# Rewriting the start of a two-layer MLP kernel: the order of ten cells written out, eight weight buffers lent by the second layer, one exchange moved to DMA

## The chip, the cores and the metric

The kernel runs on one core of a Trainium2 chip. The metric is the device time of one execution in microseconds (us). Before the change it is 1242.22 us, the median of three runs (1239.99 to 1244.42).

## The reference, cut to what matters

Three steps follow one another on 2 x 4096 rows of 192 numbers, all in float32.

```
# 1. dynamic convolution: softmax over 7 taps, per row and head (8 heads of 24)
w = exp(weight_gen - max) / sum;  x_pad = 6 zero rows, then x
x1[b,s,h,:] = sum_k w[b,s,h,k] * x_pad[b, s+k, h, :]
# 2. first MLP, ELU          w_in 192x2048, w_out 2048x192
h = x1 @ w_in;   g = where(h > 0, h, exp(min(h, 0)) - 1);   x2 = g @ w_out
# 3. second MLP, hard swish
h = x2 @ w_in2;  g = h * clip(h + 3, 0, 6) / 6;             out = g @ w_out2
```

## The kernel before, in words

**Tiling.** The 8192 rows are cut into 16 blocks of 512. A block passes through a layer in eight cells; cell q multiplies the block by 256 of the 2048 hidden columns, applies the activation and multiplies by the matching 256 rows of the output weights. There are 2 x 16 x 8 = 256 cells, and `n` counts them. Every operand is split into a high and a low part, and a product is three products (high x high, high x low, low x high). A cell writes its first product into two PSUM banks, `h` (one set of two for even cells, one for odd cells). Its second product is accumulated in `acca` and `accb` by the matmuls of cell n+3 (`LAG`).

**One cell.** TensorE: first product of cell n, second product of cell n-3 (L515). ScalarE: two activations for each of the two banks (L537, L538), then a cast of both halves to the high part `gh` (L544). VectorE: one operation per bank to finish the activation (L554), then the low part `gl` (L548, on two SBUF tiles).

**The weights of the first layer.** They are prepared while the first ten cells run (`BOOT`). They come in 16 units of 128x384, i0 to i7 of `w_in` and o0 to o7 of `w_out`. Cell q needs unit i_q, and cell q+3 needs o_q. A unit is loaded into a `raw` buffer as pairs of 32-bit words that form float64 numbers. ScalarE takes the absolute value (`begin`, L147), VectorE makes five operations of it (`s0` to `s4`, L151 to L174), ScalarE casts the high part (`high`, L169), TensorE makes three matmuls for the rest (`p5`, L180 to L182) and ScalarE casts that to the low part (`p6`, L187). There are four raw buffers (`RAWS`). Unit k+4 is loaded once `s4` of unit k has read its buffer. From cell 3 on SyncE issues such a load only behind markers (L521) that wait for matmuls of the cell.

**Order.** All engines take their instructions in the order in which the code issues them. For the first ten cells this order comes from one string of letters for each cell (`scripts`): M the matmuls, x X y Y the activation of one and the other bank, R and G the high and low part of the cell before, 0 to 4, H, P, L the steps of the one or two units of this cell's `turn`, B the masks of the next. A digit issues the same step for both units.

**Convolution.** Block 0 is shared by VectorE and GpSimd, blocks 1 and on run on GpSimd (L279 to L302) once VectorE has made the softmax; L267 is its last step. `prepare` transposes the result, and makes the high part `xh` and the low part `xl`. Then one half of the partitions must be exchanged with the other: for block 0 by ScalarE (L337) and VectorE (L342), for all others by DMA (L346).

Of the kernel before, what the change touches and what calls it, by code (L numbers as in the profile page):

```python
# [8 lines left out]
F32 = mybir.dt.float32  # L9
F32R = mybir.dt.float32r  # L10
U32 = mybir.dt.uint32
# [6 lines left out]
def kernel(  # L18
# [62 lines left out]

    WI = [{k: cpool.tile([P, NQ * UN], F32R, name=f"wi{m}_{k}") for k in "hl"} for m in range(2)]

# [6 lines left out]

    def load_w(kind, m, q):
        raw = stage.tile([P, UN, 2], U32, tag="raw", name="raw", bufs=RAWS)
        if kind == "i":
            for k in range(2):
                c = (2 * q + k) * 2 * P
                src = w_in[m][:, c:c + 2 * P].rearrange("(g p) c -> p g c", p=HP)
                dst = raw[half[k]].rearrange("p (g c) b -> p g (c b)", g=3)
                if k == 0:
# [15 lines left out]
    class Unit:  # L114


        def __init__(self, kind, m, q, k=None):
            self.kind, self.m, self.q = kind, m, q
            self.raw = load_w(kind, m, q)
            self.hw, self.lw = self.raw[:, :, 1], self.raw[:, :, 0]  # L120
            if m == 0:

                c = k % 2 * UN
                self.f, self.rr = fts[k // 2 % 2][:, c:c + UN].bitcast(U32), boot[:, k * UN:(k + 1) * UN]

        def parts(self):
            m, q = self.m, self.q
            if self.kind == "i":
                cs = slice(q * UN, (q + 1) * UN)
                return WI[m]["h"][:, cs], [(WI[m]["l"][:, cs], slice(0, UN))], lambda t: t  # L130
# [186 lines left out]
    def prepare(m, i):  # L317
# [11 lines left out]
        else:  # L329
            parts = [(zin.pop(i)[:, 0:XN], lambda t: t[:, 0])]  # L330

        def split():
            for src, w in parts:
                nc.scalar.copy(w(X["h"]), src)
            if m == 0 and i == 0:
                for a in range(2):
                    nc.scalar.copy(X["h"][half[1 - a], 1], X["h"][half[a], 0].bitcast(F32))  # L337
            for src, w in parts:
                nc.vector.tensor_tensor(w(X["l"]), src, w(X["h"]).bitcast(F32), op=ALU.subtract)
            if m == 0 and i == 0:  # L340
                for a in range(2):
                    nc.vector.tensor_copy(X["l"][half[1 - a], 1], X["l"][half[a], 0].bitcast(F32))  # L342
                return
            for k in "hl":
                for a in range(2):
                    later(1 if m == 0 and i in (1, 2) else 2, X[k][half[1 - a], 1].bitcast(F32), X[k][half[a], 0].bitcast(F32))  # L346
        return split
# [107 lines left out]
    def second_product(n, k, bank):  # L455
# [10 lines left out]
        if not bank and n + LAG < EARLY:  # L466
            ops = ops[0::2][:2] + ops[4:] + ops[1:4:2]
# [25 lines left out]
    def matmuls(n):  # L493
# [10 lines left out]
        l0, l1 = first_product(n, 0), first_product(n, 1)  # L504
        if n < EARLY:
            x1 = first_product(n + 1, 1)[:2] if n == EARLY - 1 else []
            rows = [(0, a0), (6, b0), (10 if n >= LAG else 0, l0)], [(0, l1), (9, a1), (15, b1), (19, x1)]
        else:
            x1 = first_product(n + 1, 1)[:2]
            rows = [(0, b0), (4, a0), (10, l0)], [(0, l1[2:]), (7, b1), (11, x1), (13, a1)]  # L510
        plan = [
            (s + j, k, op) for k, runs in enumerate(rows) for s, ops in runs for j, op in enumerate(ops)]
        seen = [added.pop(i) for i in range(3, NB) if n == prep[0, i] - 1]
        for _, k, (o, w, r, st, sp, wait, tell) in sorted(plan, key=lambda e: e[:2]):
# [5 lines left out]
            if tell:  # L520
# [3 lines left out]
                if now > 2 and tell[1] == 1:  # L524

                    transfers(1 + k + (now < NQ))
        if now < 3:
            transfers(len(waiting))

# [83 lines left out]
    units = [(u[0], 0, int(u[1]), k) for k, u in enumerate("i0 i1 i2 i3 o0 i4 o1 i5 o2 i6 o3 i7 o4 o5 o6 o7".split())]  # L613
    turn = [[1, 2], [3, 4], [5, 6], [7, 8], [9, 10], [11, 12], [13], [14], [15], []]
    ends = {k: n for n, ks in enumerate(turn) for k in ks} | {0: -1}
    close = [[1], [2]] + turn[1:-1]
    boards = [(aux, accb), acca, (aux, acca[1]), (aux, acca[1]), (None, None), (None, None)] + 4 * [(aux,)]
# [21 lines left out]
    begin = {i: max(7, prep[0, i - 1]) for i in range(2, NB)}  # L639
    loads = {max(2, begin[i] - 8): i for i in begin}  # L640
    softmax = {}

    three = cpool.tile([P, 1], F32, name="three")
    with tc.manual_schedule():
        nc.vector.memset(three, 3.0)
        nc.scalar.activation(warm, three, AF.Exp)
        def make(k):
            made[k] = Unit(*units[k])
# [5 lines left out]
        blk[1] = load_block(1)  # L654
        for k in (1, 2, 3):
            make(k)

        def start(n):
            for k, bank in zip(turn[n], boards[n]):
                made[k].masks(bank)  # L660

# [9 lines left out]
        for s in c0[5:]:  # L671
            s()
        c1 = attention(1)
        for s in c1[:4]:
            s()
        prepare(0, 0)()
        start(0)
        for s in c1[4:]:
            s()
        wst = Stream(wtasks)  # L680
        for n in range(len(cells) + LAG):
            now = n
            jobs = []
            if n < BOOT:
                for k in range(len(made), len(units)):
                    if ends[k - RAWS] < n:
                        make(k)
            for m, i in order:
# [4 lines left out]
                if m and i < NB - 1 and n == last[m, i] + LAG + 3:  # L693
                    jobs.append(give(i))
            if n < BOOT:
                new, old = [made[k] for k in turn[n]], [made[k] for k in close[n]]
                spare = hset[(n + 1) % 2][::-1][-len(old):] if n > 1 else [(aux, accb)[n]]
                work = {
                    "M": lambda: matmuls(n),
                    "R": lambda: round_g(n - 1), "G": lambda: rest_g(n - 1),  # L700
                    "H": lambda: [u.high() for u in new],
                    "x": lambda: act_a(n, 1), "X": lambda: gate(n, 1),
                    "y": lambda: act_a(n, 0), "Y": lambda: gate(n, 0),
                    "J": lambda: [f() for f in jobs],
                    "P": lambda: [u.p5(ps) for u, ps in zip(old, spare)],
                    "L": lambda: [u.p6() for u in old],
                    "B": lambda: start(n + 1) if n + 1 < BOOT else None}
                work |= {str(k): (lambda k: lambda: [getattr(u, f"s{k}")() for u in new])(k) for k in range(5)}
                for step in scripts[n]:
                    work[step]()  # L710
            else:
                matmuls(n)
                for k in (1, 0):
                    if n < len(cells):
                        act_a(n, k)
                        gate(n, k)
                    if not k:
                        continue
                    for b in order[:-1]:
                        if n == last[b] + LAG:  # L720
                            fold_b(*b)
                    if n <= len(cells):
                        round_g(n - 1)
                        rest_g(n - 1)
                    for b in order[:-1]:
                        if n == last[b] + LAG + 1:
                            fold_a(*b)
                for f in jobs:
                    f()
            if n == BOOT:  # L730
                want(0)
            wst.run(n)
            for i in range(2, NB):

                k = n - (begin[i] - 5) - (i == 2)
                if k == 0:
                    softmax[i] = attention(i)
                if 0 <= k < 4:
                    softmax[i].pop(0)()
                if n == begin[i]:  # L740
                    for s in softmax.pop(i):
                        s()
            if n < 3:
                transfers(len(waiting))
            if n in loads:
                blk[loads[n]] = load_block(loads[n])
        finish()
# [30 lines left out]
```

## Time and profile before

| | |
|---|---|
| median of three runs | 1242.22 us |
| profiled execution | 1237.81 us, of which the span of the core's instructions is 1236.0 |
| busy share of the span | TensorE 96%, VectorE 76%, ScalarE 69%, GpSimd 34% |
| mean granted TensorE clock | 0.991 of full speed |

All rows below are of this one execution, and times in them count from the start of its span. In a timeline row the bracket at the end is the idle time of that engine just before the instruction, and what ended it. A wait for several things is put down to the one that came last.

### The profile page before, as it was taken

The numbers are of one execution on the slowest core, as the hardware profiler recorded it, in microseconds if no ns is written. First come the engines' busy times: TensorE is split into PE (matmuls) and PEld (weight loads), VectorE is DVE, ScalarE is ACT, GpSimd is POOL, SyncE is SP. The second block draws the span as 40 slices with busy tenths as digits, with TensorE's granted clock in tenths as the row PEclk, the third lists the DMA queues.
The fourth block names the chain that finished last, engine by engine and source line by source line (L and its number), as shares of the span: only waits on it lengthen the run. The fifth ranks groups of instructions, "written<-read, shape, count | busy, mean of one in ns | idle before, by whom it ended". The sixth has DMA issues, their size and how long they took to land.

```text
span 1236.0 us, 25367 instructions
## 1 busy us (share of the span) xinstructions
PE 1191.7 (96%) x10146; PEld 946.1 (77%) x10146; DVE 938.8 (76%) x1225; ACT 856.7 (69%) x1339; POOL 416.8 (34%) x234
## 2 busy tenths in 40 slices
PE   3788999999999999999999999999999999999998
PEld 1466777777877777787788888888888888888887
DVE  7865899999999999999777666666666666666664
ACT  3656788888888888888886555566655556666554
POOL 8416877777787777778000000000000000000000
PEclk9899999999999999999999999999999999999999
DMA  5331222212222221221121011111111111111110
GB/s 135 112 103 37 88 88 88 68 43 66 88 88 88 88 66 39 71 88 53 52 65 45 21 52 52 47 45 52 33 33 53 52 50 42 53 33 33 52 40 27
DMA packets 33254, 75.03 MB, mean 61 GB/s; under 512 B 4340, under 2 KB 17010, under 8 KB 33136
## 3 DMA queue, kind: packets, MB, share of 16 engines
q1 hardware_dynamic: 32992, 73.21, 20.4%
q8 instruction: 80, 1.31, 0.4%
q14 instruction: 38, 0.31, 0.1%
q10 hardware_dynamic: 144, 0.20, 0.0%
HBM read 36.43 MB, written 12.58 MB: 40 GB/s over the span
## 4 chain that ended last, share of the span: by engine, by line
PE 92%; DVE 4%; DMA 2%; ACT 2%; issue 0%; SPq 0%; DVEq 0%; ACTq 0%
PE h L515 42%; PE acca L515 28%; PE accb L515 19%; DMA raw<-in_moe_w_out_dram 1%; DVE gl L548 1%; PE acca L327 1%; DMA xt<-in_x_dram 1%; DVE r L554 1%; ACT r L538 0%; PE acca L413 0%; ACT r L537 0%; PE acca L485 0%; DVE h L279 0%; DVE f L158 0%; PE accb L485 0%
## 5 line engine op out<-in xcount | busy, mean ns | idle before, releaser
L515 PE MATMUL h<-xh,wi_h 64*128 64x512 f32 x1536 | 566.7, 397 | 13.6 <-ACT wi_l L187 12.2
L515 PE MATMUL h<-xh,wi_l 64*128 64x512 f32 x1536 | 568.6, 397 | 0.0
L515 PE MATMUL h<-xl,wi_h 64*128 64x512 f32 x1536 | 564.3, 395 | 0.0
L515 PE MATMUL acca<-gh,wo 64*128 64x512 f32 x2024 | 560.5, 395 | 0.0
L548 DVE TENSOR_TENSOR gl<-r,gh 128x1024 fp32r<-128x1024 f32 x256 | 393.9, 1539 | 61.6 <-ACT gh L544 60.6
L515 PEld LDWEIGHTS acca<-gh,wo 64*128 64x128 f32 x2024 | 375.8, 186 | 47.9 <-issue 1.0
L540 ACT ACTIVATE r<-h,three 128x512 f32<-128x512 f32 x256 | 176.1, 688 | 222.7 <-PE h L515 113.2
L515 PE MATMUL accb<-gh,wo 64*128 64x512 f32 x1012 | 321.6, 397 | 5.5 <-ACT wo L187 5.5
L515 PEld LDWEIGHTS h<-xh,wi_h 64*128 64x128 f32 x1536 | 284.4, 187 | 52.1 <-ACT wi_l L187 13.4
L515 PE MATMUL acca<-gl,wo 64*128 64x512 f32 x1012 | 318.7, 394 | 0.0
L515 PE MATMUL accb<-gl,wo 64*128 64x512 f32 x1012 | 318.2, 394 | 0.3 <-DVE gl L548 0.3
L515 PEld LDWEIGHTS h<-xl,wi_h 64*128 64x128 f32 x1536 | 284.3, 186 | 35.7
L515 PEld LDWEIGHTS h<-xh,wi_l 64*128 64x128 f32 x1536 | 284.3, 186 | 35.5
L557 DVE SCALAR_TENSOR_TENSOR r<-r,h 128x512 f32<-128x512 f32 x256 | 175.9, 687 | 161.2 <-ACT r L540 160.4
L544 ACT CAST gh<-r 128x1024 fp32r<-128x1024 f32 x256 | 266.8, 1042 | 12.7 <-DVE r L554 11.9
L554 DVE SCALAR_TENSOR_TENSOR r<-r,h 128x512 f32<-128x512 f32 x256 | 173.3, 677 | 53.8 <-ACT r L538 52.2
L515 PEld LDWEIGHTS accb<-gh,wo 64*128 64x128 f32 x1012 | 185.8, 186 | 27.0 <-ACT wo L187 6.5
L515 PEld LDWEIGHTS accb<-gl,wo 64*128 64x128 f32 x1012 | 187.8, 186 | 24.0 <-DVE gl L548 0.7
L515 PEld LDWEIGHTS acca<-gl,wo 64*128 64x128 f32 x1012 | 188.1, 186 | 23.4
L279 POOL TENSOR_TENSOR tmp<-xt,wt 128x768 f32<-128x768 f32 (+1 forms) x95 | 189.3, 1992 | 6.1
L537 ACT ACTIVATE r<-h 128x512 f32<-128x512 f32 x256 | 152.4, 595 | 49.9 <-PE acca L515 30.6
L538 ACT ACTIVATE r<-r 128x512 f32<-128x512 f32 x256 | 162.0, 633 | 8.1
(134 smaller groups left out, 747.8 us busy)
## 6 DMA issues: line engine op xcount, KB each, us to landing
xt<-in_x_dram SPq DMA_DIRECT2D x14, 960.0 KB, 5.6
xh<-xh SPq DMA_DIRECT2D x62, 192.0 KB, 2.7
xl<-xl SPq DMA_DIRECT2D x62, 192.0 KB, 2.9
raw<-in_moe_w_out_dram SPq DMA_DIRECT2D x16, 384.0 KB, 3.3
z<-z SPq DMA_DIRECT2D x16, 384.0 KB, 2.3
zin<-z SPq DMA_DIRECT2D x16, 384.0 KB, 3.0
out_dram<-ot SPq DMA_DIRECT2D x15, 384.0 KB, 4.3
raw<-in_moe_w_in_dram SPq DMA_DIRECT2D x16, 192.0 KB, 3.4
```

The lines of the kernel that those rows point to most:

```text
L279: eng.tensor_tensor(o.rearrange("p t (h g) -> p t h g", g=G), xk, wk.rearrange("p (t h) g -> p t h g", h=H), op=ALU.mult)
L327: nc.tensor.transpose(ps[h][:, t * HP:(t + 1) * HP], src[p], ident[p, p])
L515: mm = nc.tensor.matmul(o, w, r, start=st, stop=sp).ins
L537: nc.scalar.activation(r, h, AF.Relu, scale=-1.0)
L538: nc.scalar.activation(r, r, AF.Exp, scale=-1.0)
L540: nc.scalar.activation(r, h, AF.Relu, bias=three)
L544: nc.scalar.copy(gg[n][0], rs[n])
L548: nc.vector.tensor_tensor(gl, rs.pop(n), gh.bitcast(F32), op=ALU.subtract)
L554: nc.vector.scalar_tensor_tensor(r, r, -1.0, h, op0=ALU.add, op1=ALU.max)
L557: nc.vector.scalar_tensor_tensor(r, r, 6.0, h, op0=ALU.min, op1=ALU.mult)
```

## The change

**Order.** The letters per cell are replaced by one list for the ten cells (`SCRIPT`), whose tokens name the step and its unit or cell: C5.2 is step s2 of unit 5, B5, H5, P5, L5 are its masks, high part, matmuls and low part, M4, x4, X4, y4, Y4, R4, G4 belong to cell 4, s1a to sC are softmax steps, T1, J, j are the transposes, high parts and low parts of block 1, wh and wl those of block 0. Steps of two or three units now stand in turns. `masks` and `sums` name the PSUM bank of each unit.

**Buffers.** Units 4 to 11 get buffers of their own, in the place where the second layer's input weights will lie later. The loads of units 4 to 7 are issued before cell 0, those of 8 to 11 right behind the exchange of `xl`, those of 12 to 15 at cell 2 into the four raw buffers. None stands behind a marker.

**Exchange.** The exchange of block 0's `xl` is two DMAs in SyncE's queue in place of two VectorE casts; that of `xh` stays on ScalarE.

**Matmuls.** In cells 8 and 9 the first and second product are interleaved as in the cells before them, where they followed the pattern of the later cells.

```diff
+    early = [cpool.tile([P, 4 * UN, 2], U32, tag=f"wi1{k}", name=f"early_{k}") for k in "hl"]
...
-    def load_w(kind, m, q):
-        raw = stage.tile([P, UN, 2], U32, tag="raw", name="raw", bufs=RAWS)
+    def load_w(kind, m, q, k=None):
+        if k is None or not RAWS <= k < RAWS + 8:
+            raw = stage.tile([P, UN, 2], U32, tag="raw", name="raw", bufs=RAWS)
+        else:
+            c = (k - RAWS) % 4 * UN
+            raw = early[(k - RAWS) // 4][:, c:c + UN]
...
-                for a in range(2):
-                    nc.vector.tensor_copy(X["l"][half[1 - a], 1], X["l"][half[a], 0].bitcast(F32))
...
+        def swap(keys, put):
+            for k in keys:
+                for a in range(2):
+                    put(X[k][half[1 - a], 1].bitcast(F32), X[k][half[a], 0].bitcast(F32))
...
-        if now is None or now >= len(cells) or now < 3 and n == 0:
+        if now is None or now >= len(cells) or now < BOOT and n == 0:
             nc.sync.dma_start(out, in_)
...
-    scripts = ["M012H34xXyYPLB", "MPR01xX2LyYH34GB", "MR01xX2yYH34GPLB"] + (BOOT - 3) * ["MR012H34GxXJByYPL"]
+    masks, sums = "xxbaccxcx----ccc", "xxbfbedgfedxcxxx"
+    SCRIPT = """
+        s1a B2 B1 C2.0 e1 C1.0 wh0 s1b wh1 wh2 wl0 s1c wh3 wl1 C2.1 B4 M0 C1.1 B3 C2.2 C4.0 H2 C1.2 C4.1 H1
+        C1.3 C3.0 C1.4 C4.2 P1 x0 C3.1 C4.3 C3.2 L1 M1 C4.4 y0 C2.3 X0 B5 C2.4 B6 Y0 P2 x1 C5.0 C6.0 y1 C3.3
...
+    """
...
-        for k in (1, 2, 3):
+        for k in range(1, 8):
             make(k)
...
+            elif t[:2] == "wl":
+                split[0].rest(int(t[2]))
+                if t == "wl1":
+                    split[0].swap("l", nc.sync.dma_start)
+                    for k in range(8, RAWS + 8):
+                        make(k)
```

SyncE's queue before the change: the last piece of unit 3's load, then unit 4, unit 5 in three pieces, unit 6, and so on as buffers come free.

```order
L579 DMA raw<-in_moe_w_in_dram 64x256
L579 DMA raw<-in_moe_w_out_dram 128x2x384
L579 DMA raw<-in_moe_w_in_dram 64x3x256
L579 DMA raw<-in_moe_w_in_dram 64x2x256
L579 DMA raw<-in_moe_w_in_dram 64x256
L579 DMA raw<-in_moe_w_out_dram 128x2x384
```

The same place after the change, where `early_h` holds units 4 to 7.

```order
L598 DMA raw<-in_moe_w_in_dram 64x256
L598 DMA early_h<-in_moe_w_out_dram 128x2x384
L598 DMA early_h<-in_moe_w_in_dram 64x3x256
L598 DMA early_h<-in_moe_w_in_dram 64x2x256
L598 DMA early_h<-in_moe_w_in_dram 64x256
L598 DMA early_h<-in_moe_w_out_dram 128x2x384
L598 DMA early_h<-in_moe_w_in_dram 64x3x256
L598 DMA early_h<-in_moe_w_in_dram 64x2x256
L598 DMA early_h<-in_moe_w_in_dram 64x256
L357 DMA xl<-xl 64x768 x2
L598 DMA early_l<-in_moe_w_out_dram 128x2x384
```

Three more units are loaded ahead of cell 0's end, and the exchange of `xl` stands behind them and in front of four more.

VectorE after the low parts of block 0, before the change: the two casts, then units 1 (`aux`) and 2 (`accb`) step by step.

```order
L339 TENSOR_TENSOR xl<-acca_77,xh 128x384
L342 CAST xl<-xl 64x768 x2
L151 TENSOR_SCALAR aux<-aux 128x384
L151 TENSOR_SCALAR accb<-accb 128x384
L154 TENSOR_SCALAR aux<-aux 128x384
L154 TENSOR_SCALAR accb<-accb 128x384
L158 SCALAR_TENSOR_TENSOR f<-raw,aux 128x384
L158 SCALAR_TENSOR_TENSOR f<-raw,accb 128x384
```

The same place after the change.

```order
L352 TENSOR_TENSOR xl<-acca_77,xh 128x384
L165 TENSOR_SCALAR accb<-accb 128x384
L165 TENSOR_SCALAR aux<-aux 128x384
L169 SCALAR_TENSOR_TENSOR f<-raw,accb 128x384
L162 TENSOR_SCALAR acca_77<-acca_77 128x384
L169 SCALAR_TENSOR_TENSOR f<-raw,aux 128x384
L165 TENSOR_SCALAR acca_77<-acca_77 128x384
L174 TENSOR_SCALAR aux<-f 128x384
L162 TENSOR_SCALAR acca_76<-acca_76 128x384
L185 SCALAR_TENSOR_TENSOR boot<-raw,aux 128x384
```

The casts are gone, and steps of units 4 (`acca_77`) and 3 (`acca_76`) stand between those of 1 and 2.

VectorE around the last softmax step of block 2 (L267, which lets GpSimd begin that block), before the change; the first `gl` here is cell 5's.

```order
L548 TENSOR_TENSOR gl<-r,gh 128x1024
L554 SCALAR_TENSOR_TENSOR r<-r,h_73 128x512
L554 SCALAR_TENSOR_TENSOR r<-r,h_72 128x512
L267 TENSOR_TENSOR wt<-wt,mx 128x224
L151 TENSOR_SCALAR aux<-aux 128x384
```

The same step after the change (now L278); the `gl` here is cell 3's.

```order
L352 TENSOR_TENSOR xl<-aux,xh 128x384
L573 SCALAR_TENSOR_TENSOR r<-r,h_72 128x512
L278 TENSOR_TENSOR wt<-wt,mx 128x224
L162 TENSOR_SCALAR tr<-tr 128x384 x2
L567 TENSOR_TENSOR gl<-r,gh 128x1024
```

The step stood behind the `gl` of cell 5, and now stands ahead of that of cell 3.

## Rows read from the trace of the kernel before

**Rows 1.** Windows: length, busy per engine, PEclk the granted clock, DMA share, GB/s.
```profile
40.00:50.00 10.00, 5.01 (x24) 3.50 (x25) 10.00 (x17) 7.16 (x14) 4.99 (x4) 0.66 0.55 190
20.90:116.58 95.68, 73.42 (x434) 51.45 (x436) 69.14 (x120) 59.21 (x114) 47.76 (x28) 0.89 0.25 77
181.10:217.30 36.20, 36.20 (x320) 28.89 (x318) 34.09 (x43) 30.33 (x51) 27.25 (x15) 1.00 0.25 75
```
**Rows 2.** Waits of VectorE, 20.9 to 116.6 us: total, times, longest.
```profile
DVE r L554 <- ACT r L538: 23.5, 10, 5.5
```
**Rows 3.** Timeline of VectorE: start, length, operation, idle time before it.
```profile
57.81 0.69 DVE L554 SCALAR_TENSOR_TENSOR r<-r,h 128x512 f32<-128x512 f32 x1 [2.76 <-ACT r L538]
...
70.02 0.69 DVE L554 SCALAR_TENSOR_TENSOR r<-r,h 128x512 f32<-128x512 f32 x1 [5.50 <-ACT r L538]
...
79.57 0.69 DVE L554 SCALAR_TENSOR_TENSOR r<-r,h 128x512 f32<-128x512 f32 x1 [2.54 <-ACT r L538]
...
96.95 0.69 DVE L554 SCALAR_TENSOR_TENSOR r<-r,h 128x512 f32<-128x512 f32 x1 [4.82 <-ACT r L538]
...
115.16 0.69 DVE L554 SCALAR_TENSOR_TENSOR r<-r,h 128x512 f32<-128x512 f32 x1 [3.05 <-ACT r L538]
```
**Rows 4.** Timeline of ScalarE, first and last of the masks that wait.
```profile
54.72 0.55 ACT L147 ACTIVATE tr<-raw 128x384 f32<-128x384 f32 x1 [1.54 <-DMA raw<-in_moe_w_in_dram]
...
95.22 0.52 ACT L147 ACTIVATE aux<-raw 128x384 f32<-128x384 f32 x1 [4.66 <-DMA raw<-in_moe_w_out_dram]
```
**Rows 5.** Timeline of SyncE's queue: start and length of issues.
```profile
6.47 10.65 SPq L579 DMA_DIRECT2D raw<-in_moe_w_in_dram  x9
...
50.15 2.73 SPq L588 DMA_DIRECT2D raw<-in_moe_w_in_dram  x3
```
**Rows 6.** Waits of SyncE's queue, up to 130 us.
```profile
SPq L521 <- PE acca L515: 40.1, 17, 7.3
```
**Rows 7.** Timeline of VectorE in cells 0 and 1.
```profile
22.06 2.74 DVE L342 CAST xl<-xl 64x768 fp32r<-64x768 f32 x2
...
30.60 0.69 DVE L554 SCALAR_TENSOR_TENSOR r<-r,h 128x512 f32<-128x512 f32 x1 [0.43 <-ACT r L538]
...
35.52 0.69 DVE L554 SCALAR_TENSOR_TENSOR r<-r,h 128x512 f32<-128x512 f32 x1 [1.14 <-ACT r L538]
```
**Rows 8.** Timeline of VectorE: the low part of cells 1 and 8.
```profile
47.47 1.21 DVE L548 TENSOR_TENSOR gl<-r,gh 128x1024 fp32r<-128x1024 f32 x1
...
106.69 2.62 DVE L548 TENSOR_TENSOR gl<-r,gh 128x1024 fp32r<-128x1024 f32 x1 [0.17 <-ACT gh L544]
```
**Rows 9.** Timeline of GpSimd: first and last of block 2's 14 operations, first of block 3's.
```profile
87.41 1.54 POOL L279 TENSOR_TENSOR y<-xt,wt 128x768 f32<-128x768 f32 x1 [42.26 <-DVE wt L267]
...
112.02 0.74 POOL L302 TENSOR_TENSOR y<-y,tmp 128x256 f32<-128x256 f32 x1
126.07 1.83 POOL L279 TENSOR_TENSOR y<-xt,wt 128x768 f32<-128x768 f32 x1 [13.31 <-PE aux L327]
```
**Rows 10.** Windows of the first loads.
```profile
10.00:20.00 10.00, 3.17 (x14) 1.78 (x14) 8.85 (x19) 0.87 (x2) 8.55 (x10) 1.00 0.97 213
20.00:30.00 10.00, 5.51 (x26) 3.37 (x25) 9.66 (x17) 6.13 (x12) 8.74 (x5) 0.95 0.05 15
```
**Rows 11.** DMA issues up to 170 us: KB each, median us to landing.
```profile
xl<-xl SPq DMA_DIRECT2D x4, 192.0 KB, 3.1
```
**Rows 12.** Timeline of TensorE: the weight matmuls of units 1, 2 and 15; cells 0 and 2.
```profile
21.41 0.80 PE L515 MATMUL h<-xh,wi_h 64*128 64x512 f32 x2 [0.94 <-ACT xh L334]
...
29.16 1.65 PE L180 MATMUL aux<-f,ident 128*128 128x384 f32 x2 [3.06 <-DVE boot L174]
...
34.11 0.91 PE L180 MATMUL accb<-f,ident 128*128 128x384 f32 x2
...
35.30 0.50 PE L515 MATMUL h<-xh,wi_h 64*128 64x512 f32 x2
...
110.02 0.91 PE L180 MATMUL h<-f,ident 128*128 128x384 f32 x2
```

More of the change, by code (lines that the diff above doesn't have):

```diff
@@ L330, in prepare, with cast, turn, rest @@
             parts = [(zin.pop(i)[:, 0:XN], lambda t: t[:, 0])]
-        def split():
-            for src, w in parts:
-                nc.scalar.copy(w(X["h"]), src)
-            if m == 0 and i == 0:
-                for a in range(2):
[L337 to L341, printed above, removed]
-                    nc.vector.tensor_copy(X["l"][half[1 - a], 1], X["l"][half[a], 0].bitcast(F32))
[L343 to L346, printed above, removed]
+        def cast(k):
+            src, w = parts[k]
+            nc.scalar.copy(w(X["h"]), src)
+        def turn(a):
+            nc.scalar.copy(X["h"][half[1 - a], 1], X["h"][half[a], 0].bitcast(F32))
+        def rest(k):
+            src, w = parts[k]
+            nc.vector.tensor_tensor(w(X["l"]), src, w(X["h"]).bitcast(F32), op=ALU.subtract)
+        def swap(keys, put):
+            for k in keys:
+                for a in range(2):
+                    put(X[k][half[1 - a], 1].bitcast(F32), X[k][half[a], 0].bitcast(F32))
+        def split():
+            for k in range(len(parts)):
+                cast(k)
+            for k in range(len(parts)):
+                rest(k)
+            swap("hl", lambda o, t: later(1 if (m, i) == (0, 2) else 2, o, t))
+        split.cast, split.turn, split.rest, split.swap = cast, turn, rest, swap
         return split
@@ L639 @@
     begin = {i: max(7, prep[0, i - 1]) for i in range(2, NB)}
-    loads = {max(2, begin[i] - 8): i for i in begin}
+    loads = {begin[i] - 8: i for i in begin if i > 2}
     softmax = {}
@@ L672, with products @@
             s()
[L673 to L679, printed above, removed]
+        c1, split = attention(1), {0: prepare(0, 0)}
+        def products(n):
+            nonlocal now
+            if n:
+                trail(n - 1)
+            now = n
+            if n == 2:
+                blk[2] = load_block(2)
+                for k in range(RAWS + 8, len(units)):
+                    make(k)
+            matmuls(n)
+            if n == begin[2]:
+                for s in softmax.pop(2):
+                    s()
@@ new lines, in trail, with special @@
+        def trail(n):
+            for i in range(2, NB):
+                k = n - (begin[i] - 5)
+                if i > 2 and k == 0:
+                    softmax[i] = attention(i)
+                if i > 2 and 0 <= k < 4:
+                    softmax[i].pop(0)()
+                if i > 2 and k == 5:
+                    for s in softmax.pop(i):
+                        s()
+            if n in loads:
+                blk[loads[n]] = load_block(loads[n])
+        def special(t):
+            if t == "T1":
+                split[1] = prepare(0, 1)
+            elif t in ("s1a", "e1", "s1b"):
+                c1.pop(0)()
+            elif t == "s1c":
+                for s in c1:
+                    s()
+            elif t == "J":
+                split[1].cast(0)
+                split[1].cast(1)
+            elif t == "j":
+                split[1].rest(0)
+                split[1].rest(1)
+                split[1].swap("hl", nc.sync.dma_start)
+            elif t[:2] == "wh":
+                k = int(t[2])
+                (split[0].turn if k > 1 else split[0].cast)(k % 2)
+            elif t[:2] == "wl":
[3 more added lines that the diff above has]
+                    for k in range(8, RAWS + 8):
+                        make(k)
+            else:
+                if t == "sA":
+                    softmax[2] = attention(2)
+                softmax[2].pop(0)()
@@ new lines @@
+        plain = {
+            "M": products, "R": round_g, "G": rest_g,
+            "x": lambda n: act_a(n, 1), "y": lambda n: act_a(n, 0), "X": lambda n: gate(n, 1), "Y": lambda n: gate(n, 0),
+            "H": lambda k: made[k].high(), "L": lambda k: made[k].p6(), "P": lambda k: made[k].p5(banks[sums[k]]),
+            "B": lambda k: made[k].masks(banks.get(masks[k]))}
+        for t in SCRIPT.split():
+            if t[0] == "C":
+                k, p = t[1:].split(".")
+                getattr(made[int(k)], "s" + p)()
+            elif t[0] in plain and t[1:].isdigit():
+                plain[t[0]](int(t[1:]))
+            else:
+                special(t)
@@ L680 @@
+        trail(BOOT - 1)
         wst = Stream(wtasks)
-        for n in range(len(cells) + LAG):
+        for n in range(BOOT, len(cells) + LAG):
             now = n
             jobs = []
[L684 to L687, printed above, removed]
             for m, i in order:
@@ L694 @@
                     jobs.append(give(i))
[L695 to L729, printed above, removed]
+            matmuls(n)
+            for k in (1, 0):
+                if n < len(cells):
+                    act_a(n, k)
+                    gate(n, k)
+                if not k:
+                    continue
+                for b in order[:-1]:
+                    if n == last[b] + LAG:
+                        fold_b(*b)
+                if n <= len(cells):
+                    round_g(n - 1)
+                    rest_g(n - 1)
+                for b in order[:-1]:
+                    if n == last[b] + LAG + 1:
+                        fold_a(*b)
+            for f in jobs:
+                f()
             if n == BOOT:
@@ L732 @@
             wst.run(n)
[L733 to L746, printed above, removed]
+            trail(n)
         finish()
```

45 lines of the change are left out of this document (25 added, 20 removed).

## The prediction

> **What bounds the kernel now.** I read the windows first. From 181.10 to 217.30, cells 24 to 31, TensorE is busy all 36.20 us at granted clock 1.00: eight cells at 4.53 us, and nothing but fewer matmuls would shorten them [rows 1]. The change leaves those cells alone. The stretch that it rewrites is the one from 20.90 to 116.58, from the first split of block 0 to the low part `gl` of cell 9. There TensorE is busy 73.42 of 95.68 us at a mean clock of 0.89, ScalarE 59.21, VectorE 69.14 [rows 1]. No engine is full, so an order with less waiting can be shorter, and VectorE sits idle for 95.68 - 69.14 = 26.5 us.
>
> Then the waits of VectorE: 23.5 us of that idle time, in ten pieces, stand before the last step of an activation (L554) and end with ScalarE's L538 [rows 2]. ScalarE isn't slow there, it is late. Its timeline shows it standing in front of the masks of a weight unit until the raw words land, in four cells, at 54.72 first and at 95.22 last [rows 4]; the activation behind it in the queue waits too. On VectorE these four waits are the pieces of 2.76, 5.50, 2.54 and 4.82 us, together 15.6 [rows 3].
>
> Why the words are late stands on SyncE. From cell 3 on a load is issued behind markers that wait for matmuls (40.1 us on `acca` alone, [rows 6]), and only when one of four buffers is free: unit 9 at 50.15 [rows 5], though the DMA engines were nearly unused from 20 to 30 us (15 GB/s, [rows 10]).
>
> **The change part by part.** The yardstick is the start of `gl` of cell 9, 116.58, since the 69 us of VectorE work before it are the same in both orders but for the casts. Behind it both kernels run the same order.
>
> *Loads.* Units 4 to 15 are issued without a marker, 4 to 7 before cell 0. Three more units than before come right behind one another, 3 x 0.39 MB. The engines moved 213 GB/s at a share of 0.97 from 10 to 20 us, and 0.15 MB were left after 20 [rows 10]; so these units are in by 20 + (1.18 + 0.15)/0.213 = 26 us, and the next four, 1.57 MB, by about 37 with the exchange between. The 20 steps of units 1 to 4, some 0.5 us each, fill VectorE past 30 us together with the activations of cells 0 and 1, so the words are early from there on, and the four waits go: 15.6 us less. Could they come back? Only if a unit were wanted before it is in; the tightest is unit 5 (masks behind the activations of cell 0, after 30 us).
>
> *Exchange.* The two casts held VectorE for the 2.66 us from 22.06 to the next operation at 24.72, one of 2.74 in the row [rows 7]: 2.7 less. Two DMAs take their place, and their price is a wait on TensorE: the last matmuls of cell 0 need them, and the matmuls of unit 1, the activation of cell 0 and all that is queued behind these on ScalarE and VectorE stand behind. They are issued behind units 4 to 7. The bounds: they start at 23 us, when `xl` is ready, and land at 26.1 with the 3.1 us of such a DMA [rows 11]; or they start when the units are in, and land at 29.3. Unit 1's matmuls started at 29.16 before, held by VectorE [rows 12]; without the casts they could start at 26.5. So the DMA costs between 0 and (29.3 + 1 for the last matmuls - 26.5) = 4 us. I take the middle, 2, since both the backlog and the early start are in the rows.
>
> *Order on VectorE.* Of the 23.5 us, 15.6 are the loads; 0.43 and 1.14 stand in cells 0 and 1 [rows 7]; the other 6.3 come after 79 us, and most of them end late, the last and longest (3.05, [rows 3]) at 115.16, when only few weight steps are left and VectorE waits for a TensorE that was held up by the same loads. In the new order weight steps last until cell 9's products, and TensorE isn't behind; I let the 6.3 go. The 1.6 in the first cells, and the 3.0 that are left of the 26.5, I leave: a list for three engines must wait somewhere, and the bounds are that all of it goes, or that as much comes in addition.
>
> *GpSimd's block 2.* Its first operation waits for VectorE's L267 and it runs from 87.41 to 112.76, 25.3 us [rows 9]. While it runs, `gl` takes 2.62 us (cell 8), against 1.21 without it (cell 1) [rows 8], 1.41 more. L267 stood behind the `gl` of cell 5, so three of them (cells 6 to 8) ran beside block 2; it now stands ahead of that of cell 3, so six do. Three more cost 3 x 1.41 = 4.2 us; the bounds are nothing, if they fall between GpSimd's operations, and twice that, if GpSimd is drawn out too and reaches cell 9's.
> The Trainium skill speaks against this part more sharply: "SBUF — State Buffer", section "SBUF: two separate sides", says that a VectorE operation with two SBUF inputs and a GpSimd operation share a port pair by an exclusive lock, and that the loser waits for the other's whole instruction. `gl` reads two SBUF tiles, and the 1.41 is of the size of one GpSimd operation (1.54, [rows 9]), so the trace agrees. By the lock the eight SBUF steps of units 9 to 12 can be held as well, up to 8 x 1.54 = 12 us, and the gain would be 18.4 - 12 = 6.
>
> *What is hidden.* Units' steps done in turns save VectorE nothing that counts. The two reordered cells have the same matmuls. Second-layer weights come into the lent buffers only after cell 10, when unit 11 is long done. All three at nothing; they are hidden by TensorE's and VectorE's other work, and if unit 11 were late, its steps would show it first.
>
> *The sum.* 15.6 + 2.7 + 6.3 - 2.0 - 4.2 = 18.4 us earlier at cell 9. Does it last? From cell 24 on TensorE is full, so cells come as much earlier as cell 10 does, provided that block 2 of the convolution (wanted in cell 13) and block 3 are not the next to be late: block 2 ended at 112.76 and GpSimd then waited 13.3 us for TensorE to take it [rows 9]; it now starts earlier within the order, so this slack stays. The profiled execution took 1237.81; 1237.8 - 18.4 = 1219.4. The median of the three runs lies 4.4 above that execution, and I carry this over: 1223.8.
>
> **The rivals.**
> 1. *TensorE becomes the bound.* Cells 3 to 9 take 7 x 4.53 us, cells 0 to 2 have 9 of 19 pairs of matmuls, 3 x 2.15, and the 15 units' matmuls take 35.30 - 34.11 = 1.19 each, 17.9: together 56 us from 21.41 [rows 1, 12]. Cell 10 could begin at 77.5; it began at 110.02 + 1.19 = 111.2. So the floor of a perfect list is 34 us lower. For it speaks that all 26.5 us of idle VectorE would have to go, against it that VectorE alone still has 69 - 2.7 us of work: at most 26.5 + 2.7 = 29 us of gain, 1213. A gain of 24 to 29: 1213 to 1218.
> 2. *The waits change places.* The loads' waits go, but a list that ties three engines step by step hands on every delay; the late 6.3 stay, the exchange costs its 4, block 2 its 8.4. Then 15.6 + 2.7 - 4 - 8.4 = 6, or 1236; with one of the three not so bad 7 to 13, 1229 to 1235. For it speaks that VectorE then has 69.1 - 2.7 + 8.4 = 75 us of work and ScalarE 59, in 90.
> 3. *The loads stay late.* If the one queue is held up so that units 8 to 15 are as late as before, nothing is won: 1238 to 1246. Against it: no marker stands ahead of them, and the engines were idle.
> 4. *Slower: TensorE stays at its low clock.* From 40 to 50 us, with TensorE idle half of the time, the granted clock was 0.66 [rows 1], that is 1.2 GHz for most of it. If the new list makes short waits in every cell, TensorE can stay there. The 56 us at a mean clock c take 56/c; they reach the 111.2 - 21.4 = 89.8 us of before at c = 0.62, and below that the kernel is slower: at 0.55 by 102 - 90 = 12 us, 1254. Against it: with much idle time the mean was 0.89 [rows 1]. "TensorE: Matmul & The Clock Gate", section "HAM oscillation", of the Trainium skill says that bursts of matmuls between waits can each begin cold, which is this rival's mechanism; the trace shows it in that one stretch.
>
> **How the numbers follow.** The forecast, a gain of 13 to 24: 0.60. Rival 1: 0.10. Rival 2: 0.18. Rival 3: 0.06. Rival 4: 0.06. The best case of the bounds adds 2 + 4.2 + 4.6 to 18.4, beyond rival 1's limit of 29, so the low end is 1213; the upper end takes in rival 2 up to 1236, which leaves out rivals 3 and 4 and a little of the two ends. A measurement of this kernel can't tell less than about 0.3%, 3.7 us, from no change. Faster: 0.60 + 0.10 + 0.17 = 0.87; same: the rest of rival 2 and most of rival 3, 0.06; slower: 0.07.
>
> **What would show it.** Right: no wait of ScalarE for `raw` after 30 us; `gl` of cell 9 near 98; VectorE idle about 10 us up to it; the DMAs of `xl` landing between 26 and 29.5; `gl` of cells 3 to 8 at 2 us and more; an unchanged 36 us for eight cells later. Wrong: waits for `raw` that persist (rival 3), a granted clock under 0.7 up to cell 10 (rival 4), or waits of VectorE for ScalarE that add up to 20 us with no load behind them (rival 2).

## The result and the profile after

The changed kernel takes 1227.59 us, the median of four runs (1226.06 to 1228.03), against 1241.87 for the kernel before beside it (four runs, 1239.99 to 1244.42). The ratio is 0.9881, with a 95% interval of 0.9862 to 0.9901: 14.3 us faster. The two profiled executions are 1237.81 and 1227.44, which is 10.4 apart; the kernel before scatters by several us, and its profiled execution was one of the quicker ones. All that follows about where time went is on the scale of the profiled executions.

The low part `gl` of cell 9 starts at 105.94 instead of 116.58, 10.64 us earlier, and the last cell's is as much earlier (10.54). The whole difference is made in the first ten cells, and nothing is given back later.

Windows of the changed kernel; columns as in [rows 1], which they answer.

```profile
20.90:105.94 85.04, 69.71 (x434) 46.31 (x436) 75.62 (x122) 58.11 (x114) 48.28 (x28) 0.96 0.35 93
20.00:30.00 10.00, 4.20 (x18) 2.27 (x18) 9.40 (x22) 5.62 (x11) 6.40 (x5) 1.00 1.07 243
30.00:40.00 10.00, 9.26 (x45) 5.66 (x46) 5.92 (x13) 6.80 (x14) 9.61 (x6) 1.00 1.09 292
62.57:80.47 17.90, 10.14 (x53) 6.14 (x51) 17.90 (x18) 7.13 (x14) 16.97 (x10) 0.87 0.36 106
177.00:213.20 36.20, 36.20 (x320) 28.90 (x318) 34.12 (x43) 30.33 (x50) 27.29 (x15) 1.00 0.25 76
```

Read the first row against the 95.68 us of before. VectorE was idle for 26.5 us and is now idle for 85.04 - 75.62 = 9.4: 17.1 us less, close to what was forecast. But it is busy for 75.62 us instead of 69.14, though the two casts of 2.7 us are gone. So some 9 us of VectorE work have appeared that no instruction was added for (0.9 us of it are four softmax steps of block 1, which ran ahead of 20.90 before). The fourth row says where to look: from 62.57 to 80.47 VectorE is busy without a gap, with only 18 instructions, while TensorE has work for 10.14 of 17.90 us.

The timeline of VectorE in that stretch (start, length, operation; between the two `gl` stand the steps of units 11, 12 and 13, x2 is two steps in one row, `tr` is a mask tile in SBUF, `acca` one in PSUM):

```profile
63.11 2.57 DVE L567 TENSOR_TENSOR gl<-r,gh 128x1024 fp32r<-128x1024 f32 x1
65.59 3.62 DVE L165 TENSOR_SCALAR tr<-tr 128x384 uint32<-128x384 uint32 x2
69.14 1.90 DVE L169 SCALAR_TENSOR_TENSOR f<-early_l,tr 128x384 uint32<-128x384 uint32 x1
70.96 0.55 DVE L162 TENSOR_SCALAR acca<-acca 128x384 f32<-128x384 f32 x1
71.42 1.70 DVE L169 SCALAR_TENSOR_TENSOR f<-raw,tr 128x384 uint32<-128x384 uint32 x1
73.04 0.55 DVE L165 TENSOR_SCALAR acca<-acca 128x384 uint32<-128x384 uint32 x1
73.51 1.23 DVE L174 TENSOR_SCALAR tr<-f 128x384 uint32<-128x384 uint32 x1
74.66 0.54 DVE L169 SCALAR_TENSOR_TENSOR f<-raw,acca 128x384 uint32<-128x384 uint32 x1
75.13 1.71 DVE L185 SCALAR_TENSOR_TENSOR boot<-early_l,tr 128x384 fp32r<-128x384 uint32 x1
76.76 0.55 DVE L174 TENSOR_SCALAR acca<-f 128x384 uint32<-128x384 uint32 x1
77.22 1.23 DVE L174 TENSOR_SCALAR tr<-f 128x384 uint32<-128x384 uint32 x1
78.38 0.54 DVE L185 SCALAR_TENSOR_TENSOR boot<-raw,acca 128x384 fp32r<-128x384 uint32 x1
78.84 1.70 DVE L185 SCALAR_TENSOR_TENSOR boot<-raw,tr 128x384 fp32r<-128x384 uint32 x1
81.06 1.96 DVE L567 TENSOR_TENSOR gl<-r,gh 128x1024 fp32r<-128x1024 f32 x1
```

The same four operations (L165, L169, L174, L185) stand here with either tile, turn by turn: with `acca` they take 0.55, with `tr` 1.2 to 1.9. Beside them GpSimd is at block 2, whose first and last operation are these (the bracket is the idle time before it; L278, which the block needs too, had ended at 62.65):

```profile
62.87 1.72 POOL L290 TENSOR_TENSOR y<-xt,wt 128x768 f32<-128x768 f32 x1 [15.89 <-PE accb L536]
...
88.54 0.73 POOL L313 TENSOR_TENSOR y<-y,tmp 128x256 f32<-128x256 f32 x1
```

In the kernel before, block 2 ran from 87.41 [rows 9], and no step on `tr` stood beside it.

The waits that the loads made are gone. ScalarE waits for raw words once, before cell 0, where before it stood in four cells [rows 4]. Waits of ScalarE from 15 us to cell 9 (total, times, longest):

```profile
ACT accb L158 <- DMA raw<-in_moe_w_in_dram: 7.0, 1, 7.0
```

VectorE's wait for L538, now L557, falls from 23.5 us [rows 2] to 7.1 (its waits in the same form):

```profile
DVE r L573 <- ACT r L557: 7.1, 6, 2.6
```

The exchange shows in two places. One is the landing of its DMAs (DMA issues: KB each, median us from issue to landing):

```profile
xl<-xl SPq DMA_DIRECT2D x2, 192.0 KB, 6.0
```

The other is TensorE's timeline, which waits for them at the end of cell 0, with unit 1's matmuls behind:

```profile
30.65 1.22 PE L536 MATMUL h<-xl,wi_h 64*128 64x512 f32 x4 [4.42 <-DMA xl<-xl]
31.81 1.65 PE L191 MATMUL aux<-f,ident 128*128 128x384 f32 x2
```

They take 6.0 us, not the 3.1 of [rows 11]. DMA engines that were idle from 20 to 30 us [rows 10] are full through both windows above, and a run below with fewer loads ahead of the exchange tests whether that is why. Unit 1's matmuls start at 31.81, before at 29.16 [rows 12].

### The profile page after: what moved, and what is told of

It reads as the page before. It is cut to its first block, busy times and chain, and to the rows that moved or that the text cites. A ratio compares the mean times of both kernels' runs of the same rounds, so it can differ in the third digit from the quotient of the medians.

```text
span 1225.6 us, 25362 instructions
## 1 busy us (share of the span) xinstructions
PE 1188.1 (97%) x10146; PEld 941.7 (77%) x10146; DVE 944.3 (77%) x1223; ACT 856.4 (70%) x1339; POOL 417.6 (34%) x234
## 4 chain that ended last, share of the span: by engine, by line
PE 91%; DVE 2%; ACT 0%; DMA 0%; issue 0%; SPq 0%
PE h L536 42%; PE acca L536 28%; PE accb L536 19%; DVE gl L567 1%; PE acca L338 1%; PE acca L432 0%; DVE r L573 0%; PE acca L504 0%; DVE boot L185 0%; PE accb L504 0%; DVE tr L174 0%; DMA xl<-xl 0%; ACT gh L563 0%; PE aux L191 0%; DVE tr L185 0%
## 5 line engine op out<-in xcount | busy, mean ns | idle before, releaser
L563 ACT CAST gh<-r 128x1024 fp32r<-128x1024 f32 x256 | 266.6, 1042 | 13.3 <-DVE r L573 12.5
L557 ACT ACTIVATE r<-r 128x512 f32<-128x512 f32 x256 | 162.0, 633 | 8.1
```

Source lines behind the costliest of these rows:

```text
L557: nc.scalar.activation(r, r, AF.Exp, scale=-1.0)
L563: nc.scalar.copy(gg[n][0], rs[n])
```

## The experiments

My theory after this reading: the gain fell short because VectorE's steps on SBUF tiles are held while GpSimd runs block 2, and, for a smaller part, because the exchange waits behind seven units of weights. The rivals: transfers into SBUF slow the steps; or the order itself waits elsewhere, and the loads alone were worth more. Each kernel is timed against the kernel before beside it (1241.87 for the changed kernel, 1240.88 for the next four rows, 1240.43 for the last four). Between rows of different groups a difference of 1 us or so says nothing. Every reading of a trace is of one execution of its kernel.

| kernel | median us | ratio to before, 95% | start of `gl` of cell 9 |
|---|---|---|---|
| changed kernel | 1227.59 | 0.9881 [0.9862, 0.9901] | 105.94 |
| late block 2 | 1216.28 | 0.9804 [0.9784, 0.9824] | 96.35 |
| exchange first | 1225.58 | 0.9877 [0.9857, 0.9897] | 105.11 |
| loads only | 1225.24 | 0.9874 [0.9854, 0.9895] | 103.97 |
| order only | 1231.89 | 0.9925 [0.9909, 0.9942] | 110.63 |
| late block 2 and exchange first | 1211.43 | 0.9763 [0.9738, 0.9789] | 89.56 |
| late block 2, exchange by casts | 1215.33 | 0.9795 [0.9770, 0.9819] | 93.76 |
| order only, late block 2 | 1221.77 | 0.9843 [0.9819, 0.9867] | 100.06 |
| unit 11's masks in PSUM | 1222.52 | 0.9852 [0.9827, 0.9877] | 101.09 |

**Late block 2.** One token moves: the last softmax step of block 2, on which GpSimd waits, from cell 5 to the front of cell 7's matmuls.

```
-        ... P9 B13 sC C11.0 C12.0 G3 P10 ...
+        ... P9 B13 C11.0 C12.0 G3 P10 ...
-        X6 M7 R5 C14.0 ...
+        X6 sC M7 R5 C14.0 ...
```

> The changed kernel with one token moved: the last softmax step of block 2 (which lets GpSimd begin that block) stands right ahead of cell 7's matmuls, behind the last SBUF steps of units 9 to 12. Theory 1: in the changed kernel GpSimd's block 2, from 62.9 to 89.3 us, holds VectorE's steps on SBUF tiles (two L165 take 3.62 us where two alone take 0.62) and three gl; the SBUF steps lost 9.9 us, the gl 3.1. Moved, the SBUF steps cost 0.27 to 0.47 us each again, and four gl of cells 5 to 8 lose 1.2 each: gain 9.9 + 3.1 - 4.8 = 8 us, 1219 to 1221; TensorE no longer idle from 70 to 80. Rival: it was the DMA writes of x for block 3 and of the exchanges (166 GB/s from 60 to 70 us) that slowed SBUF: then the steps stay slow and the time stays within 1.5 us of 1227.6.

It is 11.3 us faster than the changed kernel, and 9.6 on the profiled executions, where the theory had 8. Block 2 starts at 73.71, and the same steps on `tr` ahead of it are short (timeline of VectorE), where with block 2 beside them they took 3.62, 1.90, 1.70, 1.23 and 1.71:

```profile
64.91 0.62 DVE L165 TENSOR_SCALAR tr<-tr 128x384 uint32<-128x384 uint32 x2
65.45 0.55 DVE L169 SCALAR_TENSOR_TENSOR f<-early_l,tr 128x384 uint32<-128x384 uint32 x1
...
66.39 0.55 DVE L169 SCALAR_TENSOR_TENSOR f<-raw,tr 128x384 uint32<-128x384 uint32 x1
...
67.32 0.35 DVE L174 TENSOR_SCALAR tr<-f 128x384 uint32<-128x384 uint32 x1
...
68.05 0.55 DVE L185 SCALAR_TENSOR_TENSOR boot<-early_l,tr 128x384 fp32r<-128x384 uint32 x1
```

The window of the same 17.90 us says the rest: TensorE is full and its granted clock 1.00, where it was 0.87, and the DMA engines move as much as in the changed kernel (107 against 106 GB/s).

```profile
62.57:80.47 17.90, 17.90 (x122) 12.57 (x120) 16.30 (x31) 14.40 (x30) 6.60 (x4) 1.00 0.35 107
```

So it isn't the transfers that slow the steps. The changed kernel says the same by itself: its DMA engines were nearly idle from 70 to 80 us, at 25 GB/s, and the steps on `tr` there were as slow as those ahead of 70 (its windows):

```profile
70.00:80.00 10.00, 2.80 (x7) 1.50 (x7) 10.00 (x11) 5.09 (x9) 9.61 (x6) 0.79 0.06 25
```

The price of a later block 2 is small: `gl` of cells 5 to 9 now runs beside it (1.66, 2.82, 2.25, 2.32 and 1.39 us), 4.3 us over five times 1.22.

**Unit 11's masks in PSUM.** The sharpest test of the same theory leaves order, loads and the start of block 2 alone, and changes where one unit's masks lie.

```
-    masks, sums = "xxbaccxcx----ccc", "xxbfbedgfedxcxxx"
+    masks, sums = "xxbaccxcx--x-ccc", "xxbfbedgfedxcxxx"
```

> The changed kernel with one letter different: the masks of unit 11 lie in a PSUM bank (aux) instead of an SBUF tile. Order, loads and the start of block 2 stay. Theory (a VectorE step is held by GpSimd only if all its operands lie in SBUF): unit 11's steps beside block 2 take 0.55 us as unit 13's do there, where its four took 1.8, 1.9, 1.2 and 1.7; with 0.24 more for the first, which had run at 0.31 ahead of GpSimd, that is 4.2 us less: 1223.5, unless unit 12's steps are held longer in turn (1225.5). Rival (the steps are slow for another reason, transfers into SBUF or the new sequence of steps): unit 11's steps stay at 1.2 to 1.9 and the time at 1227.6.

It is 5.1 us faster than the changed kernel, 1 us more than the theory's 4.2. Block 2 runs from 62.06. Unit 11 (`early_l`, `aux`) is no longer held, unit 12 (`raw`, `tr`) still is; in VectorE's timeline one reads both side by side:

```profile
66.23 0.55 DVE L165 TENSOR_SCALAR aux<-aux 128x384 uint32<-128x384 uint32 x1
66.70 1.52 DVE L165 TENSOR_SCALAR tr<-tr 128x384 uint32<-128x384 uint32 x1
68.14 0.54 DVE L169 SCALAR_TENSOR_TENSOR f<-early_l,aux 128x384 uint32<-128x384 uint32 x1
...
69.08 0.96 DVE L169 SCALAR_TENSOR_TENSOR f<-raw,tr 128x384 uint32<-128x384 uint32 x1
...
71.35 0.54 DVE L185 SCALAR_TENSOR_TENSOR boot<-early_l,aux 128x384 fp32r<-128x384 uint32 x1
...
73.95 1.71 DVE L185 SCALAR_TENSOR_TENSOR boot<-raw,tr 128x384 fp32r<-128x384 uint32 x1
```

So it is the place of the operands beside a running GpSimd that makes the steps long, not the order. The Trainium skill, "SBUF — State Buffer", section "SBUF: two separate sides", has this as an exclusive lock: a VectorE operation with two SBUF inputs, or one in a two-port mode, and a GpSimd operation hold a shared pair of ports for the whole of an instruction, and the other waits. The runs agree in size: a held step waits 0.9 to 1.5 us, less than the 1.72 of block 2's first operation. They show it for the two-input steps L169 and L185, and also for the one-input steps L165 and L174; whether these two run in a two-port mode no row says.

**Exchange first.** Units 5 to 7 are loaded behind the exchange instead of ahead of it.

```
-        for k in range(1, 8):
+        for k in range(1, 5):
...
-                    for k in range(8, RAWS + 8):
+                    for k in range(5, RAWS + 8):
```

> The changed kernel with the exchange of xl in SyncE's queue ahead of the loads of units 5 to 7, and no other difference. Theory 1: the exchange landed at 30.5 us since it queued behind 1.2 MB of loads, TensorE waited 4.4 us for it and the activations of cell 0 with it (VectorE 2.6 and 1.4 us); now it lands at 26 to 27, and the kernel gains 2.5 to 4 us: about 1224. Rival: VectorE fills that time with steps of units 1 to 4, which must be done anyway, and makes up for the rest: within 1 us of 1227.6.

TensorE's wait for `xl` shrinks to 0.74, and unit 1's matmuls start 3.3 us earlier:

```profile
27.34 1.22 PE L536 MATMUL h<-xl,wi_h 64*128 64x512 f32 x4 [0.74 <-DMA xl<-xl]
28.49 1.65 PE L191 MATMUL aux<-f,ident 128*128 128x384 f32 x2
```

The exchange, issued at 23.64 behind four units, is there at 27.34, after 3.7 us. So most of the excess of 6.0 over 3.1 came from the backlog of seven units.

But the kernel is only 2.0 us faster than the changed one, between theory and rival; as ratios to the kernel before, 0.9877 and 0.9881, the two can't be told apart. `gl` of cell 9 comes only 0.8 earlier. The collision doesn't take the lead: block 2 starts earlier too, at 59.82, the steps meet it again, and `gl` of cell 4 behind them starts 3.06 earlier than the 81.06 of the changed kernel:

```profile
78.00 1.96 DVE L567 TENSOR_TENSOR gl<-r,gh 128x1024 fp32r<-128x1024 f32 x1
```

It is lost behind the collision. The lead is still 3.07 at `gl` of cell 5 and 0.84 at that of cell 6. In between TensorE, which had been idle for most of the time from 70 to 80, has work again all the time, but at a lower granted clock than in the changed kernel: 0.75 against 0.86 (windows of this run, then of the changed kernel).

```profile
80.00:90.00 10.00, 9.99 (x56) 7.50 (x58) 7.17 (x11) 5.71 (x11) 6.03 (x4) 0.75 0.01 2
80.00:90.00 10.00, 9.36 (x57) 6.06 (x58) 9.93 (x13) 5.95 (x12) 8.96 (x6) 0.86 0.00 1
```

Why the clock stayed low longer here isn't shown.

**Late block 2 and exchange first.** Both edits together.

> Both edits together: the last softmax step of block 2 (token sC) stands in front of the matmuls of cell 7, and the exchange of xl stands in the queue behind four units instead of seven. Theory (the gain was lost to VectorE steps held beside GpSimd, and a smaller part to the exchange behind the backlog): with the collision gone nothing eats the 2.3 us that the earlier exchange won at cell 0, so the two edits add up: 1216.3 - 2.3 = 1214, with gl of cell 9 near 94. Rival (from cell 3 on VectorE's own work sets the pace, and what is won at cell 0 becomes a wait later): no better than the late block 2 alone, 1216.

In time they more than add up: 1211.43 is 16.2 us below the changed kernel and 4.9 below the late block 2 alone, where the theory had 2.3. This is the best version that I ran. TensorE hardly waits for `xl` (its timeline):

```profile
26.12 1.22 PE L536 MATMUL h<-xl,wi_h 64*128 64x512 f32 x4 [0.33 <-DMA xl<-xl]
27.27 0.91 PE L191 MATMUL aux<-f,ident 128*128 128x384 f32 x2
```

From 20.90 to just behind cell 9's `gl` it is busy 68.11 of 71.00 us (windows):

```profile
20.90:91.90 71.00, 68.11 (x454) 47.04 (x456) 66.35 (x119) 59.25 (x115) 47.17 (x26) 1.00 0.38 110
```

Unit 1's matmuls also take 0.91 here and 1.65 in all other runs, and they aren't alone: TensorE's pace changes at this point. In this run the matmuls from here on are short; in exchange first a pair of matmuls behind unit 1's takes 0.63 where it takes 0.40 here, and 0.91 is reached only with unit 2's matmuls (timeline of TensorE, this run, then exchange first):

```profile
28.80 0.40 PE L536 MATMUL h<-xl,wi_h 64*128 64x512 f32 x2
30.76 0.91 PE L191 MATMUL accb<-f,ident 128*128 128x384 f32 x2
```
```profile
31.30 0.63 PE L536 MATMUL h<-xl,wi_h 64*128 64x512 f32 x2
34.36 0.91 PE L191 MATMUL accb<-f,ident 128*128 128x384 f32 x2
```

From unit 1's matmuls to unit 2's it is 3.49 us here and 5.87 there. These 2.4 us are nearly the whole 2.6 by which this run beat the theory's 1214, so the surplus is no proof that the two edits help each other. Why the pace changes earlier here stays open: the granted clock of the windows around is 1.00 in both.

**Late block 2, exchange by casts.** The exchange of `xl` by two VectorE casts, as before the change.

```
-                    split[0].swap("l", nc.sync.dma_start)
+                    for a in range(2):
+                        nc.vector.tensor_copy(split[0].X["l"][half[1 - a], 1], split[0].X["l"][half[a], 0].bitcast(F32))
```

> Late block 2 as before, and the exchange of xl made by two VectorE casts again, as in the kernel before; the loads of units 8 to 11 keep their place. It prices the exchange in the new order without the collision. Theory of the prediction (2.7 us of casts against 2.0 of waiting): 0.7 us slower than the late block 2 alone, 1217. Rival (the DMAs land at 30 us and TensorE waits 5.1 us for them, so they cost 4 or more): faster by 1.3 to 2 us, 1214 to 1215, with no wait of TensorE for xl over 1 us and gl of cell 0 earlier than 41.

1215.33 against 1216.28: the casts are as good as DMAs behind seven units, or 1 us better (the intervals of the two ratios overlap), and 3.9 us worse than DMAs behind four. The theory's 1217 is missed; the time lies just above the rival's 1214 to 1215, and its two signs came, a wait of 0.62 and `gl` of cell 0 at 40.11. TensorE no longer waits for the exchange, but for VectorE, which has the casts to do ahead of unit 1's steps:

```profile
26.21 1.22 PE L536 MATMUL h<-xl,wi_h 64*128 64x512 f32 x4 [0.62 <-DVE xl L748]
30.52 1.65 PE L191 MATMUL aux<-f,ident 128*128 128x384 f32 x2 [3.09 <-DVE boot L185]
```

**Loads only.** The kernel before with eight lent buffers and early loads; its order and its casts stay.

```
-        for k in (1, 2, 3):
+        for k in range(1, 8):
...
+        for k in range(8, RAWS + 8):
+            make(k)
```

> The kernel before with the loads alone changed: units 4 to 11 in the eight lent buffers, 4 to 7 loaded before cell 0, 8 to 11 right behind block 0's split, 12 to 15 in cells 0 to 2; order of the engines and the exchange by VectorE's casts as before. Theory 1 (late loads were the bound): the four waits of 15.6 us go, and with them most of the 6.3 us later: gain 14 to 20, so 1222 to 1228, as much as the whole change or more, since here GpSimd's block 2 meets no SBUF step. Rival (the written order is what counts): gain under 7, 1235 or more.

1225.24, as the theory had it: as good as the whole change. The waits for raw words are gone, and this order starts block 2 at 79.84, behind the steps on `tr`. What it keeps are the late waits (timeline of VectorE), which answer to the last of [rows 3]:

```profile
98.81 0.69 DVE L565 SCALAR_TENSOR_TENSOR r<-r,h 128x512 f32<-128x512 f32 x1 [1.84 <-ACT r L549]
102.55 0.69 DVE L565 SCALAR_TENSOR_TENSOR r<-r,h 128x512 f32<-128x512 f32 x1 [3.06 <-ACT r L549]
```

**Order only.** The changed kernel with four raw buffers, each load issued as soon as its buffer has been read, with no marker ahead of it.

```
-        if k is None or not RAWS <= k < RAWS + 8:
+        if True:
...
+                if p == "4":
+                    read.add(int(k))
+                    while len(made) < len(units) and len(made) - RAWS in read:
+                        make(len(made))
```

> The changed kernel without the lent buffers: its order and its exchange by DMA, but four raw buffers, each load issued as soon as its buffer has been read. Theory 1 (late loads were the bound): ScalarE waits for raw words again, 10 us and more in sum, and the gain against the kernel before is at most 5 us: 1237 or more. Rival (the written order is what counts): within 3 us of the changed kernel's 1227.6.

1231.89, 9 us faster than before: between theory and rival, and neither has it. Issued without markers, loads are late less often: ScalarE waits 7.9 us for raw words after cell 0 began, against 13.5 in the kernel before, and 5.6 of it in two waits (waits of ScalarE: total, times, longest):

```profile
ACT acca L158 <- DMA raw<-in_moe_w_out_dram: 2.9, 1, 2.9
ACT tr L158 <- DMA raw<-in_moe_w_in_dram: 2.7, 1, 2.7
ACT tr L158 <- DMA raw<-in_moe_w_out_dram: 1.7, 2, 0.9
ACT aux L158 <- DMA raw<-in_moe_w_out_dram: 0.6, 1, 0.6
```

**Order only, late block 2.** The same with `sC` late.

> The new order with four raw buffers, each load issued as soon as its buffer is read, and block 2 late. Without the late block 2 this took 1231.9. Theory (SBUF steps beside GpSimd cost some 10 us in any order that puts them side by side): 1221 to 1223, and what is left to the 1216.3 of the kernel with the early loads is what the lent buffers are worth in this order, 5 to 6 us. Rival (its time is set by the two waits for raw that are left, 5.6 us in sum, and the collision falls into them): 1229 to 1232.

1221.77: the collision cost this order 10.1 us, as the theory has it. The two longest waits for raw words stay as they were (3.0 and 2.8), so they didn't hide it. What lies between 1221.77 and the 1216.28 with early loads, 5.5 us, is the lent buffers' worth in this order.

## Why the prediction was right, and where it failed

The time, 1227.6 against 1223.8, lies in the range and the direction is right. The gain was put 4.1 us too high in medians (18.4 against 14.3) and 8.0 too high on the profile's own scale (10.4). That the time is off by 4 us and not by 8 is luck: I carried the 4.4 us between profile and median over to the new kernel, and its profiled execution was at its median. In medians the gain lies just inside the forecast's 13 to 24; on the profile's scale, where the terms were worked out, it lies below, in rival 2's 7 to 13.

*Loads (15.6): right that they were late, too large by itself.* No wait for raw words is left after cell 0. Alone, the loads took 15.6 us off the median, but 12.6 off the start of `gl` of cell 9, which was the yardstick; the first agreement is partly chance. And they aren't worth as much in every order: with the new order and loads issued without markers, the lent buffers bring 4 to 6 us.

*Late waits (6.3): about half, and the cause partly wrong.* I laid the longest of them to loads. With early loads and the old order two of 1.84 and 3.06 stay, so they are the order's. In the new order 3.0 of VectorE's 7.1 us of waiting come after 79 us, in four pieces, none over 1.1.

*Casts and exchange (2.7 less, 2.0 more): mis-sized on TensorE, nearly right on VectorE.* The upper bound for landing was 29.3; TensorE's last matmuls of cell 0 started at 30.65. By the term, unit 1's matmuls would start at 28.5; they started at 31.81, 3.3 later, 0.6 of which is that cell 0 began later (22.03 against 21.41). VectorE's waits in cells 0 and 1 grew from 1.6 to 4.1, by 2.5. The forecast gain of 0.7 for the whole edit wasn't seen; with the late block 2 the casts are even with the DMAs or 1 us better. 4.9 us more could have been had with three units moved behind the exchange, of which 2.4 are TensorE's faster pace in that one run.

*GpSimd's block 2 (4.2): the step that failed.* I counted three more `gl` beside it, six in all, at 1.41 each. Only three stood beside it, as before, and they cost nothing more: before, those of cells 6 to 8 were held by 3.1 us over 1.22 each, now those of cells 3 to 5 by as much. What was held instead are eight steps of units 11 and 12 on SBUF tiles: L165, L169, L174 and L185, 13.1 us in the rows above and 3.5 in the same steps with block 2 later, so 9.6 us. They were named in the prediction, with 12 us as the most, and left out of the sum; in the trace of before no step on `tr` stood beside GpSimd's block 2, so there was no row to price one. The sentence on the lock, with its gain of 6, was the better guide to the place; the gain of 10.4 lies between it and mine.

*The account.* `gl` of cell 9 was expected at 98.2 and came at 105.94, 7.8 later. By its terms VectorE would have been busy for 69.1 - 2.7 + 4.2 = 70.6 us and idle for 26.5 - 15.6 - 6.3 + 2.0 = 6.6; it was busy for 75.6 and idle for 9.4. (The sign "VectorE idle about 10 us" doesn't fit these terms, so that it came is no support for them.) The 5.0 us of work too much are 5.8 for steps held beside GpSimd (9.6 on SBUF tiles and 0.4 for `gl`, most of it cell 0's, instead of 4.2) and 0.9 for softmax steps of block 1, less 1.7 in other steps; 1.0 of that is steps on PSUM tiles, whose standing in turns had been put at nothing. The 2.8 of idle time are 3.0 of late waits and 0.5 at the exchange, less 0.7 elsewhere.

*Signs.* Three came: no wait for raw words after 30 us, VectorE idle about 10, 36 us for eight later cells. Three didn't: `gl` of cell 9 near 98, the exchange landing by 29.5, and `gl` of cells 6 to 8 at 2 us and more (they took 1.23).

*Rivals.* TensorE didn't become the bound, but in the best version it nearly did: `gl` of cell 9 came 27 us earlier than before, and rival 1 had put the most at 29. Rival 2 came nearest, and in part by its own mechanism: about half of the late waits stay, and block 2 costs 9.6 us where it had 8.4, though on other operations. The loads didn't stay late. The granted clock rose, from 0.89 to 0.96 in the mean, so rival 4 fell; from 62.57 to 80.47, where TensorE had work for 57% of the time, it was 0.87.

*Lasting:* right. Eight cells take 36.20 us as before, and GpSimd's earlier block 2 brings nothing later on.

## What to carry to other kernels

Where an order is rewritten, list for each engine what now stands beside what, above all VectorE steps whose operands all lie in SBUF beside GpSimd: a trace of the old order can't show a collision that it didn't have. If a consumer of a GpSimd result has slack (here 13.3 us of waiting [rows 9]), start GpSimd later, or put one operand into PSUM. An exchange by DMA is priced by what is queued ahead of it, not by its time on idle engines; put what isn't urgent behind it. And follow a gain cell by cell to the end of the stretch: 3 us won at cell 0 were still there behind the collision and lost two cells later.

## What the runs showed that I had not expected

- One held VectorE step costs 0.9 to 1.5 us more, however short it is: `TENSOR_SCALAR` on `tr` of 128x384 takes 0.31 alone (two in 0.62) and 1.2 to 1.8 beside GpSimd, `f<-raw,tr` 0.55 and 1.7 to 1.9. With the mask in PSUM it is 0.55 in both cases.
- GpSimd hardly suffers from the short steps: block 2 took 62.87 to 89.27 with the collision, 26.4 us, and 25.3 before. With block 2 late, where `gl` of five cells stand beside it, it took 28.5 (73.71 to 102.21).
- The two DMAs of `xl`, issued when the loads of units 4 to 7 had gone out in the 5 us ahead of them, land after 6.0 us instead of 3.1, and the rate rises from 213 GB/s [rows 10] to 243 and 292 while they and the loads run.
